# Three kinds of element-wise work moved between GpSimd, ScalarE and VectorE in a fused attention and two-MLP kernel

## The chip, the cores and the metric

The kernel runs on one core of a Trainium2 chip. Measured is the device time of one execution in microseconds (us). The engines: TensorE (PE in the profile, its weight loads PEld), VectorE (DVE), ScalarE (ACT), GpSimd (POOL), and SP, whose queue issues most of the DMAs. Each engine works through its own instructions in the order in which the program gives them, and waits at one until what it needs is there.

## The reference

Three stages, all in fp32: gated linear attention, a mixture of 8 experts with one expert per token, and a dense MLP over all 3072 tokens.

```python
# attention: B=4, H=8, S=768, D=48
f = 1.0 / (1.0 + np.exp(-f_logit))
for t in range(S):
    state = f[:, :, t, :, None] * state + np.einsum('bhd,bhe->bhde', k[:, :, t], v[:, :, t])
    y[:, :, t] = np.einsum('bhd,bhde->bhe', q[:, :, t], state)

# first experts: x (3072, 384), E=8, F=1024; only tokens with x @ w_skip > 0
logits = xc @ w_gate
e_idx = np.argmax(logits, axis=1)
for e in range(E):
    h = np.maximum(xc[mask] @ w1[e], 0.0)
    y[mask] = gate_w[mask, None] * (h @ w2[e])
out[do_compute] = xc + y

# second MLP: F=2048
h = x @ w_in
sp = log1p(exp(h))
g = h * np.tanh(sp)
return g @ w_out
```

## The kernel before, in words

TensorE multiplies in fp32r, a rounded form of fp32. To keep precision every operand is split into a rounded part (hi) and a residual (lo = raw - hi), and each product is three matmuls: hi*hi, hi*lo, lo*hi. So beside TensorE there is much element-wise work: rounding copies and residual subtractions, of the weights (the class `Weights`), of the transposed inputs (`transposed`) and of the hidden values (`split`, `gate`).

*Weights.* They come from HBM by DMA into three stage buffers, a chunk at a time. `Weights.step` handles one piece: for the first experts a chunk has three pieces of 512 columns. ScalarE casts the piece to hi (L123); the residual of the piece before (L108, in `flush`) is issued on the engine that the caller passes in, VectorE if none. With the last piece of a chunk the residual of that piece follows at once, and a new chunk is asked for. The second MLP's weights are wide (64 bit) and need three VectorE instructions more per piece (L129 to L131); their residual is L108 or L135.

*The first experts* (`moe`). Expert 0 is computed in two halves of 128 tokens: `half1` multiplies with the tokens as the stationary operand, `half2` transposes the result back on TensorE and splits it, `layer2` makes the second product. Between them `steps(n)` handles n pieces of weights for later experts. From s = 8 on a loop runs over s = (expert e, slice f of 128 hidden columns): `layer1` for s (L890), `layer2` for s - 3 (L905), at f = 5 and 6 the transposes of the next expert's rows (`make_xT`; one PSUM buffer pt, L849, read by ScalarE in L850 and VectorE in L851), and up to two pieces of weights. `split` (L878 on ScalarE, L879 on VectorE: mhh and mhl) reads each h from PSUM.

*The second MLP* (`moe2`, the second experts). `order` is a list of 96 steps (block b of 512 tokens, slice f of 128 hidden columns); the first 32 steps are blocks 0 and 1. In step s the code issues `layer1` for s (9 matmuls of 512 columns, L1056; three PSUM buffers h), `gate` for s - 5, `read_h` for s, and `layer2` for s - 7 (12 matmuls of 384 columns, L1105). `read_h` copies h out of PSUM to hs (L1068) and starts the activation with a sigmoid on ScalarE; `tanh_sp` does the logarithm and tanh for two or four steps in one go, with a table load before each kind. `gate` makes hs * sp (L1086), its rounded part gh (L1087) and its residual gl (L1088). In steps 3 to 6 the four pieces of block 1's input are transposed, each through pt (L849), with cast and residual on VectorE (L850, L851). Only GpSimd issues the indirect scatters (L224): rows of the first experts, and the four output pieces at the end of a block.

*Which engine.* In `moe`, pieces alternated between VectorE and GpSimd for the residual. In `moe2`, `busy(b, f)` was true for the first 32 steps: there ScalarE copied h and VectorE made gl; later VectorE copied h and GpSimd made gl.

Of the kernel before, what the change touches and what calls it, by code (L numbers as in the profile page):

```python
# [8 lines left out]
F32 = mybir.dt.float32  # L9
# [5 lines left out]
ALU = mybir.AluOpType  # L15
# [842 lines left out]
def moe(tc, A, st, weights, expert_w, pools, work, ps, ys2, rows0, xT0, x0, attn, more, first):  # L858
    nc = tc.nc
# [5 lines left out]
    def load_x(e):  # L865
        xin[e] = load_rows(tc, A, pools, NTOK + e * CAP)
# [29 lines left out]
    def layer2(e, f, halves):  # L896
        _, (w2h, w2l) = expert_w[e]
        weights.need(2 * e + 1, (f + 1) * DM)
        for a in halves:
            if f == 0:  # L900
                ys[e, a] = ys2[e % 2]().tile([128, DM], F32, name="y", tag=f"y{e % 2}", bufs=2)
            hh, hl = hts.pop((e, f, a))
            ws = slice(f * DM, (f + 1) * DM)
            for i, (h, w) in enumerate(((hh, w2h), (hh, w2l), (hl, w2h))):
                nc.tensor.matmul(  # L905
                    ys[e, a], lhsT=h, rhs=w[:, ws],
                    start=(f == 0 and i == 0), stop=(f == NE - 1 and i == 2),
                )
# [3 lines left out]
    def half1(a, g, k, hi, lo, spare):  # L912
        (w1h, w1l), _ = expert_w[0]
        weights.need(0, 4 * (g + 1) * KD * 128)
        if k == 0:
            rows_of[a, g] = ps.tile([128, 512], F32, name="h", tag="h", bufs=3)
        h = rows_of[a, g]
        for i, (w, x) in enumerate(((w1h, hi), (w1h, lo), (w1l, hi))):
            nc.tensor.matmul(  # L919
                h, lhsT=x[:, k, :], rhs=w.rearrange("p (f k t) -> p k f t", k=KD, t=128)[:, k, 4 * g:4 * g + 4, :],  # L920
                start=(k == 0 and i == 0), stop=(k == KD - 1 and i == 2),
            )
        if k == KD - 1:
            r = rows_of[a, g] = spare()
            nc.scalar.copy(r, h)

    def half2(a, g):
        h = ps.tile([128, 512], F32, name="h", tag="h", bufs=3)
        r = rows_of.pop((a, g))
        for i in range(4):  # L930
            nc.tensor.transpose(h[:, i * 128:(i + 1) * 128], r[:, i * 128:(i + 1) * 128], ident)
        for i in range(2):
            hts[0, 4 * g + 2 * i, a], hts[0, 4 * g + 2 * i + 1, a] = split(h[:, i * CAP:(i + 1) * CAP])

    def finish(e, halves):
        for a in halves:
            x = xin[e][:, a, :]
            nc.vector.scalar_tensor_tensor(x[:, 0:DM], ys[e, a], x[:, GATE:GATE + 1], x[:, 0:DM], ALU.mult, ALU.add)
            scatter_rows(tc, "experts", st, U[0:NTOK, :], x[:, POS:POS + 1].bitcast(U32), x)
# [7 lines left out]
    NF = FF // 128  # L947
    LAG = 3
    both = (0, 1)

    def steps(n):
        for i in range(n):
            weights.step(nc.gpsimd if i % 2 else None)

    x0 = (*st["x0T"], st["spare"])
    half1(0, 0, 0, *x0)
# [18 lines left out]
    for f in range(NF):  # L975
        if f == 3:
            half2(0, 1)
            steps(4)
        layer2(0, f, (0,))
    finish(0, (0,))  # L980
    make_xT(0, 1)
    make_xT(1, 0, "h", 3)
    make_xT(1, 1, "h", 3)
    steps(4)
    x1 = [t[:, :, 128:256] for t in xT[0]]
    for g, k in ((0, 0), (0, 1), (0, 2), (1, 0), (1, 1), (1, 2)):
        half1(1, g, k, *x1, spare)
        if (g, k) == (1, 1):
            half2(1, 0)
    for f in range(NF):  # L990
# [7 lines left out]
    for s in range(NF, total + 1):  # L998
        e, f = divmod(s, NF)
        if s < total:  # L1000
            layer1(e, f)
        if s >= NF + LAG:
            e2, f2 = divmod(s - LAG, NF)
            if s < total:
                layer2(e2, f2, both)
                if f2 == NF - 1:
                    finish(e2, both)
                    if e2 + 3 < NE:
                        load_x(e2 + 3)
            else:  # L1010
                for a in both:
                    for f2 in range(NF - LAG, NF):
                        layer2(e2, f2, (a,))
                    if a == 0:
                        first_rows(1)
                    finish(e2, (a,))
                weights.step(nc.gpsimd)
                first()
            if (e, f) == (NE - 1, LAG):
                for j in range(3):  # L1020
                    rows0[j] = load_rows(tc, A, pools, 256 * j)
        if e + 1 < NE and f in (5, 6):
            make_xT(e + 1, f - 5)
        if (e, f) == (NE - 1, NF - 1):
            first_rows(0)
        for i in range(1 if e == 1 and f in (3, 4, 5, 6) else 2):
            if weights.unit() < 2 * min(e + 3, NE):
                weights.step(nc.gpsimd if s % 2 else None)
            elif i == 0 and (NE - 2) * NF <= s < total - 1 and s % 4 < 3:
                weights.step()  # L1030


def moe2(tc, A, st, weights, w2, pools, work, ps, ys2, xTs, rows0):
    nc = tc.nc
# [3 lines left out]
    NF = FF2 // 128  # L1038
    BATCH = 4
    GLAG = 5  # L1040
    LAG = 7
    HF = NF // 2
    order = [(b, f) for h in range(2) for b in range(2) for f in range(h * HF, (h + 1) * HF)]
# [14 lines left out]
                    start=(k == 0 and i == 0), stop=(k == KD - 1 and i == 2),  # L1058
                )

    def busy(b, f):
        return b < 2

    def read_h(b, f):
        h = hp.pop((b, f))
        hs = work.tile([128, TB], F32, name="hs", tag="hs", bufs=7)
        sp = work.tile([128, TB], F32, name="sp", tag="sp", bufs=7)
        (nc.scalar.copy if busy(b, f) else nc.vector.tensor_copy)(hs, h)  # L1068
        nc.scalar.activation(out=sp, in_=hs, func=AF.Sigmoid, scale=-1.0)  # L1069
        hts[b, f] = (hs, sp)  # L1070

# [10 lines left out]
    def gate(b, f):  # L1082
        hs, sp = hts.pop((b, f))
        gh = work.tile([128, TB], F32R, name="gh", tag="gh", bufs=4)
        gl = work.tile([128, TB], F32R, name="gl", tag="gl", bufs=3)
        nc.vector.tensor_tensor(hs, hs, sp, ALU.mult)  # L1086
        nc.vector.tensor_copy(gh, hs)  # L1087
        (nc.vector if busy(b, f) else nc.gpsimd).tensor_tensor(gl, hs, gh.bitcast(F32), ALU.subtract)  # L1088
        gs[b, f] = (gh, gl)

    def layer2(b, fs):
# [44 lines left out]
    steps = NBK * NF  # L1136
    n_test = len(weights.wide_chunks())
    for s in range(-1, steps + LAG):
        if s < 0:
            layer1(0, 0)  # L1140
            work = yield
            rows[0] = rows0[0:2]
            load_block(0)
            load_block(1)
            continue
        b, f = order[s] if s < steps else (NBK, 0)
        if 0 < s < steps:
            layer1(b, f)
        if 0 <= s - GLAG < steps:
            gate(*order[s - GLAG])  # L1150
        if s < steps:
            read_h(b, f)
            if s in (1, 3, steps - 3, steps - 1):
                tanh_sp(s - 1, 2)
            elif s % BATCH == BATCH - 1:
                tanh_sp(s - BATCH + 1, BATCH)
        if LAG <= s < steps + LAG - 2:
            layer2(order[s - LAG][0], [order[s - LAG][1]])
        if s == steps + LAG - 1:
            layer2(NBK - 1, [NF - 2, NF - 1])  # L1160
        if s == 0:
            weights.flush(nc.gpsimd)
        if s == HF - 1 or s >= HF and s % HF != HF - 1:
            weights.step(nc.gpsimd, now=True)
        if s >= 2 * NF and s < steps:
            i, at = divmod(s - 2 * NF, 3)
            if i < n_test and at == 0:
                assert not weights.left() and weights.pend is None
                weights.reload(i)
            elif i < n_test and at == 2:  # L1170
                weights.test(i)
        if s == 2 * NF + 3 * n_test + 1:
            bad = check_values(tc, st, work, weights.stage[2])
        elif s == 2 * NF + 3 * n_test + 3:
            finish_flag(tc, st, ps, work, bad)
        if s < steps:
            nb = 1 if s < HF else b + 1 if s >= 3 * HF else NBK
            at = XT_AT[0] if s < 2 * NF else XT_AT[1]
            if s == NF + 2:
                load_block(2)  # L1180
            if nb < NBK:
                if nb > 2 and f == 5:
                    load_block(nb)
                elif s % HF in at[0:4] and s < HF or nb > 1 and f in (at[4:8] if b == 1 else at):
                    i = at[0:4].index(s) if nb == 1 else at[4:8].index(f) if b == 1 else at.index(f)
                    transposed(
                        tc, st, ps, rows[nb][i // 2][:, i % 2, :], *xTs[nb % 2], slice(i * 128, (i + 1) * 128),
                        copy=nc.vector.tensor_copy,
                    )
# [383 lines left out]
```

## Time and profile before

| what | value |
|---|---|
| three runs | 746.18, 746.66, 751.29 us; median 746.66 |
| profiled execution | 747.82 us; span 746.1 us; mean granted TensorE clock 0.977 |
| TensorE (PE) busy | 715.2 us (96%) |
| VectorE (DVE) busy | 502.8 us (67%) |
| ScalarE (ACT) busy | 508.9 us (68%) |
| GpSimd (POOL) busy | 317.1 us (43%) |

The attention part ends near 178 us, the first experts near 322 us, the second MLP's last matmul near 737 us. The busy table averages over these parts. A line of a timeline gives the start in us, the time taken, the engine, the line and the operation, how many instructions are merged, and in brackets how long the engine had been idle before and what ended that. A wait is put down to the semaphore that came last.

### The profile page before, as it was taken

Reading aid. Unit: us, or ns where it says so; the run is one execution under the profiler, and the core shown is the slowest. Engines: PE = TensorE matmul, PEld = TensorE weight load, DVE = VectorE, ACT = ScalarE, POOL = GpSimd, SP = SyncE. Lnnn points to the kernel's source line nnn. Section 1 sums busy time; section 2 is a strip of 40 time slices with the busy share of each in tenths; the row PEclk is TensorE's granted clock in tenths of the full one; section 3 lists DMA queues with packets and bytes.
Section 4 is the critical chain, followed back from the end, with each engine's and each line's share of the span. In section 5 each row is a group of like instructions: output and inputs, shape, how many; then the busy total and the mean of one; then the engine's idle time right before and its main releaser. Section 6 shows DMA issues by size and latency. Waiting matters only on the chain.

```text
span 746.1 us, 12713 instructions
## 1 busy us (share of the span) xinstructions
PE 715.2 (96%) x4749; PEld 630.0 (84%) x4749; DVE 502.8 (67%) x963; ACT 508.9 (68%) x898; POOL 317.1 (43%) x333
## 2 busy tenths in 40 slices
PE   7999999989999999998999999999999999999995
PEld 3677777667999899987989899899989998898995
DVE  6687967975666767956889886565467544666461
ACT  5788686733666664379788767767787677667681
POOL 4655675663677663120323121432253325224434
PEclk8899999987999999999999999999999999999998
DMA  9999995243788785441223011312132124100001
GB/s 185 213 207 277 234 292 145 87 156 133 218 257 276 248 257 203 145 171 43 85 86 127 1 54 62 140 43 86 43 127 85 50 90 151 50 1 33 11 1 46
DMA packets 39285, 95.50 MB, mean 128 GB/s; under 512 B 3540, under 2 KB 28160, under 8 KB 39216
## 3 DMA queue, kind: packets, MB, share of 16 engines
q1 hardware_dynamic: 35120, 82.71, 39.6%
q0 software_dynamic: 4096, 11.90, 4.3%
q8 instruction: 39, 0.64, 0.4%
q14 instruction: 30, 0.25, 0.1%
HBM read 79.53 MB, written 15.84 MB: 128 GB/s over the span
## 4 chain that ended last, share of the span: by engine, by line
PE 73%; DVE 10%; ACT 7%; DMA 4%; issue 3%; POOL 2%; SPq 0%; POOLq 0%; DVEq 0%; ACTq 0%
PE y L1105 25%; PE h L1056 24%; PE y L905 6%; PE h L890 6%; DVE fb L292 2%; PE ou L431 2%; PE fin L475 2%; PE ou L424 2%; PE pt L849 2%; PE at L373 1%; PE h L919 1%; POOL out L224 1%; DVE g L346 1%; DVE kg L345 1%; DMA kq<-in_kqT 1%
## 5 line engine op out<-in xcount | busy, mean ns | idle before, releaser
L1088 POOL TENSOR_TENSOR gl<-hs,gh 128x512 fp32r<-128x512 f32 x64 | 83.5, 1309 | 157.6 <-DVE gh L1087 131.0
L1086 DVE TENSOR_TENSOR hs<-hs,sp 128x512 f32<-128x512 f32 x96 | 90.9, 947 | 32.7 <-ACT sp L1080 32.7
L1069 ACT ACTIVATE sp<-hs 128x512 f32<-128x512 f32 x96 | 59.6, 628 | 77.3 <-DVE hs L1068 76.1
L1056 PE MATMUL h<-wB,wA 128*128 128x512 f32 x432 | 108.0, 396 | 3.2 <-ACT hs L1068 3.2
L1056 PE MATMUL h<-wB,wB 128*128 128x512 f32 x432 | 109.1, 397 | 0.0
L1105 PE MATMUL y<-wA,gh 128*128 128x384 f32 x384 | 98.4, 337 | 0.0
L1105 PE MATMUL y<-wD,gh 128*128 128x384 f32 x384 | 98.0, 336 | 0.0
L1056 PEld LDWEIGHTS h<-wB,wA 128*128 128x128 f32 x432 | 80.5, 188 | 18.2 <-ACT hs L1068 3.7
L1056 PEld LDWEIGHTS h<-wB,wB 128*128 128x128 f32 x432 | 79.5, 188 | 14.6
L1068 DVE COPY hs<-h 128x512 f32<-128x512 f32 x64 | 44.2, 691 | 67.9 <-PE h L1056 64.5
L1105 PEld LDWEIGHTS y<-wA,gh 128*128 128x128 f32 x384 | 70.8, 190 | 4.4
L1105 PEld LDWEIGHTS y<-wD,gh 128*128 128x128 f32 x384 | 70.0, 188 | 3.7
L1105 PE MATMUL y<-wA,gl 128*128 128x384 f32 x192 | 65.1, 339 | 1.6 <-POOL gl L1088 1.6
L1105 PE MATMUL y<-wD,gl 128*128 128x384 f32 x192 | 64.6, 336 | 0.0
L1076 ACT ACTIVATE sp<-sp,tiny 128x512 f32<-128x512 f32 x96 | 61.8, 713 | 0.3
L1087 DVE CAST gh<-hs 128x512 fp32r<-128x512 f32 x96 | 52.7, 549 | 3.7
L1080 ACT ACTIVATE sp<-sp 128x512 f32<-128x512 f32 x96 | 52.9, 621 | 0.3
L879 DVE SCALAR_TENSOR_TENSOR mhl<-h,mhh 128x256 fp32r<-128x256 f32 x64 | 26.7, 420 | 32.3 <-ACT mhh L878 32.0
L878 ACT ACTIVATE mhh<-h 128x256 fp32r<-128x256 f32 x64 | 24.6, 384 | 34.7 <-PE h L890 25.3
L373 PE MATMUL at<-qh,kh 48*128 48x128 f32 x384 | 35.4, 303 | 4.9 <-POOL qh L359 1.6
L387 POOL TENSOR_SCALAR_AFFINE_SELECT am<-am 128x512 f32<-128x512 f32 x41 | 29.1, 711 | 21.7 <-ACT am L385 21.0
L1105 PEld LDWEIGHTS y<-wA,gl 128*128 128x128 f32 x192 | 36.3, 189 | 2.2 <-POOL gl L1088 2.2
(238 smaller groups left out, 1544.4 us busy)
## 6 DMA issues: line engine op xcount, KB each, us to landing
stage<-in_w SPq DMA_DIRECT2D x64, 768.0 KB
kq<-in_kqT SPq DMA_DIRECT2D x6, 1344.0 KB
rows<-tokens SPq DMA_DIRECT2D x18, 388.0 KB
fb<-in_fT SPq DMA_DIRECT2D x7, 672.0 KB
vb<-in_v SPq DMA_DIRECT2D x7, 576.0 KB
tokens<-zeros SPq DMA_DIRECT2D x4, 776.0 KB
kq<-in_kqT SPq DMA_DIRECT2D x4, 448.0 KB
kq<-in_kqT SPq DMA_DIRECT2D x1, 896.0 KB
```

Source lines behind the costliest of these rows:

```text
L373: nc.tensor.matmul(at[:, j, a * CH:(a + 1) * CH], lhsT=k[r, p, :], rhs=q[r, p, :], start=True, stop=True)
L890: nc.tensor.matmul(h, lhsT=w[:, o:o + 128], rhs=x[:, k, :], start=(k == 0 and i == 0), stop=(k == KD - 1 and i == 2),)
L905: nc.tensor.matmul(ys[e, a], lhsT=h, rhs=w[:, ws], start=(f == 0 and i == 0), stop=(f == NE - 1 and i == 2),)
L1056: nc.tensor.matmul(h, lhsT=w[:, o:o + 128], rhs=x[:, k, :], start=(k == 0 and i == 0), stop=(k == KD - 1 and i == 2),)
L1068: (nc.scalar.copy if busy(b, f) else nc.vector.tensor_copy)(hs, h)
L1069: nc.scalar.activation(out=sp, in_=hs, func=AF.Sigmoid, scale=-1.0)
L1076: nc.scalar.activation(out=sp, in_=sp, func=AF.Ln, bias=st["tiny"])
L1080: nc.scalar.activation(out=sp, in_=sp, func=AF.Tanh, scale=-1.0)
L1086: nc.vector.tensor_tensor(hs, hs, sp, ALU.mult)
L1087: nc.vector.tensor_copy(gh, hs)
L1088: (nc.vector if busy(b, f) else nc.gpsimd).tensor_tensor(gl, hs, gh.bitcast(F32), ALU.subtract)
L1105: nc.tensor.matmul(ys[b][a], lhsT=g[:, a * 128:(a + 1) * 128], rhs=w, start=(first and i == 0), stop=(fs[-1] + 1 in ends and i == len(ins) ...
```

## The change

In `moe`, no caller passes GpSimd any more, so all weight residuals of the loop and of `steps` go to VectorE. Two of the four pieces handled in expert 0's first half are handled later, in the second half. In `moe2`, `gl` is always VectorE's, and `busy` depends on the step: true from step 7 to step 31, so the copies of h in steps 0 to 6 go from ScalarE to VectorE.

```diff
@@ moe
     def steps(n):
         for i in range(n):
-            weights.step(nc.gpsimd if i % 2 else None)
+            weights.step()
...
         if f == 3:
             half2(0, 1)
-            steps(4)
+            steps(2)
         layer2(0, f, (0,))
...
         half1(1, g, k, *x1, spare)
+        if (g, k) == (1, 0):
+            steps(2)
         if (g, k) == (1, 1):
             half2(1, 0)
...
             if weights.unit() < 2 * min(e + 3, NE):
-                weights.step(nc.gpsimd if s % 2 else None)
+                weights.step()
@@ moe2
-    def busy(b, f):
-        return b < 2
-
-    def read_h(b, f):
+    def busy(s):
+        return LAG <= s < 2 * NF
+
+    def read_h(s):
+        b, f = order[s]
         h = hp.pop((b, f))
...
-        (nc.scalar.copy if busy(b, f) else nc.vector.tensor_copy)(hs, h)
+        (nc.scalar.copy if busy(s) else nc.vector.tensor_copy)(hs, h)
...
-        (nc.vector if busy(b, f) else nc.gpsimd).tensor_tensor(gl, hs, gh.bitcast(F32), ALU.subtract)
+        nc.vector.tensor_tensor(gl, hs, gh.bitcast(F32), ALU.subtract)
...
-            read_h(b, f)
+            read_h(s)
```

What this does to an engine's order stands best in three places. (Lines behind the change are numbered 3 higher.)

VectorE at the start of the second MLP (wt is a wide piece of weights; pt is the transposed input, wB its place). Before:

```order
L131 SCALAR_TENSOR_TENSOR wt<-stage_81,wt 128x384
L850 CAST wB_1577<-pt 128x3x128
L851 TENSOR_TENSOR wB_1577<-pt,wB_1577 128x3x128
L850 CAST wB_1577<-pt 128x3x128
L851 TENSOR_TENSOR wB_1577<-pt,wB_1577 128x3x128
L1086 TENSOR_TENSOR hs<-hs,sp 128x512
L1087 CAST gh<-hs 128x512
L1088 TENSOR_TENSOR gl<-hs,gh 128x512
L850 CAST wB_1577<-pt 128x3x128
L851 TENSOR_TENSOR wB_1577<-pt,wB_1577 128x3x128
```

And now:

```order
L131 SCALAR_TENSOR_TENSOR wt<-stage_81,wt 128x384
L1071 COPY hs<-h 128x512 x4
L850 CAST wB_1577<-pt 128x3x128
L851 TENSOR_TENSOR wB_1577<-pt,wB_1577 128x3x128
L1071 COPY hs<-h 128x512
L850 CAST wB_1577<-pt 128x3x128
L851 TENSOR_TENSOR wB_1577<-pt,wB_1577 128x3x128
L1089 TENSOR_TENSOR hs<-hs,sp 128x512
L1090 CAST gh<-hs 128x512
L1091 TENSOR_TENSOR gl<-hs,gh 128x512
L1071 COPY hs<-h 128x512
L850 CAST wB_1577<-pt 128x3x128
```

Seven copies of h now stand in VectorE's queue, the last three each in front of a transposed piece's cast and residual; ScalarE's queue has lost them.

GpSimd behind the second block's outputs (out is the scatter of a finished block, idx the row numbers of a later one):

```order
-L1088 TENSOR_TENSOR gl<-hs,gh 128x512 x15
-L1134 COPY idx<-rows 128x2 x2
-L1088 TENSOR_TENSOR gl<-hs,gh 128x512
+L1137 COPY idx<-rows 128x2 x2
 L224 DMA out<-stage_79,idx 3072x384
 L224 DMA out<-stage_80,idx 3072x384
 L224 DMA out<-stage_79,idx 3072x384
 L224 DMA out<-stage_80,idx 3072x384
```

All 64 gl instructions are gone from GpSimd; the scatters and index copies stay.

VectorE in expert 0's two halves (wC and wD are weights of a later expert, x the first half's output, mxT transposed rows):

```order
+L108 TENSOR_TENSOR wC_2385<-stage_80,wC_2384 128x512
+L938 SCALAR_TENSOR_TENSOR x_2120<-y,x_2120 128x384
+L851 TENSOR_TENSOR mxT_2443<-pt,mxT_2442 128x3x128
+L851 TENSOR_TENSOR mxT_2451<-pt,mxT_2450 128x3x128 x2
 L108 TENSOR_TENSOR wC_2385<-stage_80,wC_2384 128x512 x2
-L938 SCALAR_TENSOR_TENSOR x_2120<-y,x_2120 128x384
-L851 TENSOR_TENSOR mxT_2448<-pt,mxT_2447 128x3x128
-L851 TENSOR_TENSOR mxT_2456<-pt,mxT_2455 128x3x128 x2
-L108 TENSOR_TENSOR wC_2385<-stage_81,wC_2384 128x512
+L108 TENSOR_TENSOR wC_2385<-stage_81,wC_2384 128x512 x3
+L108 TENSOR_TENSOR wD_2377<-stage_79,wD_2376 128x512
 L879 SCALAR_TENSOR_TENSOR mhl<-h,mhh 128x256 x4
```

One residual stands in front of x where two stood, and six stand between the transposed rows and the first mhl where one stood.

## Rows read from the trace of the kernel before

**Rows 1.** TensorE's timeline, 238 to 634 us: start, us taken, instructions merged, idle before.

```profile
245.81 0.55 PE L849 MATMUL pt<-ident,rows 128*128 128x128 f32 x3 [1.85 <-DVE mxT L851]
...
322.74 8.41 PE L1056 MATMUL h<-wB,wA 128*128 128x512 f32 x36
...
334.77 2.33 PE L1056 MATMUL h<-wB,wA 128*128 128x512 f32 x9 [0.89 <-ACT hs L1068]
...
342.16 3.06 PE L1056 MATMUL h<-wB,wA 128*128 128x512 f32 x9 [2.34 <-ACT hs L1068]
...
348.01 2.24 PE L1056 MATMUL h<-wB,wA 128*128 128x512 f32 x9
...
352.17 2.23 PE L1056 MATMUL h<-wB,wA 128*128 128x512 f32 x9
...
555.17 2.33 PE L1056 MATMUL h<-wB,wB 128*128 128x512 f32 x9
...
559.76 2.21 PE L1056 MATMUL h<-wB,wB 128*128 128x512 f32 x9
...
623.48 2.33 PE L1056 MATMUL h<-wB,wB 128*128 128x512 f32 x9
...
627.71 0.44 PE L1105 MATMUL y<-wA,gl 128*128 128x384 f32 x1 [1.55 <-POOL gl L1088]
...
629.54 2.25 PE L1056 MATMUL h<-wB,wB 128*128 128x512 f32 x9
```

**Rows 2.** Windows, TensorE: length, busy (count), granted clock, DMA share, GB/s.

```profile
343.00:347.00 4.00, 4.00 (x14) 0.57 0.30 75
```

**Rows 3.** Timelines of VectorE and GpSimd, 238 to 246 us.

```profile
240.00 4.96 DVE L108 TENSOR_TENSOR wA<-stage,wA 128x512 fp32r<-128x512 f32 x1 [0.77 <-ACT wA L123]
...
238.11 3.81 POOL L108 TENSOR_TENSOR wD<-stage,wD 128x512 fp32r<-128x512 f32 x3
241.86 2.54 POOL L108 TENSOR_TENSOR wA<-stage,wA 128x512 fp32r<-128x512 f32 x2
```

**Rows 4.** ScalarE's timeline, 312 to 352 us.

```profile
341.54 0.56 ACT L1068 COPY hs<-h 128x512 f32<-128x512 f32 x1
```

**Rows 5.** VectorE's timeline, 312 to 352 us.

```profile
331.51 0.56 DVE L850 CAST wB<-pt 128x384 fp32r<-128x384 f32 x1 [6.44 <-PE pt L849]
...
334.99 0.68 DVE L1086 TENSOR_TENSOR hs<-hs,sp 128x512 f32<-128x512 f32 x1
```

**Rows 6.** By line: count, ns least/median/most of one, first and last start, forms.

```profile
L108 DVE TENSOR_TENSOR wA<-stage,wA x11: 677/685/4956, 199.5 to 250.9; 128x512 fp32r<-128x512 f32 x11
...
L1088 DVE TENSOR_TENSOR gl<-hs,gh x32: 691/693/1533, 336.2 to 466.2; 128x512 fp32r<-128x512 f32 x32
...
L1068 DVE COPY hs<-h x64: 682/692/693, 451.6 to 720.6; 128x512 f32<-128x512 f32 x64
```

**Rows 7.** Timelines of VectorE and GpSimd, 612 to 634 us.

```profile
618.58 0.43 DVE L1087 CAST gh<-hs 128x512 fp32r<-128x512 f32 x1
...
619.76 1.30 POOL L1088 TENSOR_TENSOR gl<-hs,gh 128x512 fp32r<-128x512 f32 x1
...
626.38 3.76 POOL L1088 TENSOR_TENSOR gl<-hs,gh 128x512 fp32r<-128x512 f32 x3
```

**Rows 8.** The page's slices: busy tenths of VectorE in 40 slices of 18.7 us.

```profile
DVE  6687967975666767956889886565467544666461
```

**Rows 9.** Timelines of VectorE and TensorE in expert 0's second half.

```profile
188.12 0.68 DVE L108 TENSOR_TENSOR wC<-stage,wC 128x512 fp32r<-128x512 f32 x1
191.49 0.42 DVE L879 SCALAR_TENSOR_TENSOR mhl<-h,mhh 128x256 fp32r<-128x256 f32 x1 [2.69 <-ACT mhh L878]
...
191.97 0.44 PE L905 MATMUL y<-wB,mhl 128*128 128x384 f32 x1
```

**Rows 10.** One round: all engines (PE, PEld, DVE, ACT, POOL); then line 108 (DVE, POOL).

```profile
211.18:228.68 17.50, 17.50 (x128) 17.43 (x128) 10.80 (x20) 11.99 (x27) 13.73 (x12) 1.00 0.73 255
...
211.18:228.68 17.50, 5.76 (x7) 11.74 (x10) 1.00 0.73 255
```

## The prediction, made before the result was known

> **What bounds the kernel now.** I read the busy table first, then TensorE's own timeline for every gap behind the attention part, then the timelines of the engine that each gap names. From 200 us to the tail TensorE is the bound: it runs back to back, and only what makes it wait, or slows its clock, counts. The reader is to see in [rows 1] where its queue breaks. A normal step of the second experts (first layer, then second layer of an older step) takes 352.17 - 348.01 = 4.16 us, so 2.08 a layer. Four places are longer. Before 245.81 it waits for a residual of VectorE's (1.85). Before 334.77 and 342.16 it waits for ScalarE's copy of h (0.89, 2.34). From 555.17 to 559.76 a step takes 4.59, and from 623.48 to 629.54 another takes 6.06, the latter with 1.55 named as a wait for GpSimd's gl. The idle figures are counted from a matmul's modelled end, about 0.2 later than the queue could have gone on, so I price by starts where I can. [rows 2] is the price of the second gap besides the waiting: the mean granted clock of 343 to 347 us is 0.57, so TensorE sat at the lower level (1.2 GHz), after the idle of 0.89 and 2.34, for a loss of 4 x 0.43 = 1.7 us.
>
> **The change part by part.**
>
> *Residuals of the first experts, all on VectorE.* [rows 3]: one residual that takes 0.68 alone took 4.96 from 240.00 to 244.96, while GpSimd ran three residuals and then two, to 244.40. VectorE did not start work until GpSimd let go; the residual of the transposed rows behind it came late, and the one pt buffer held up the next transposes. With GpSimd's residuals gone that blocking has no cause. Gain: the 1.85 and the 0.2 hidden in its count, 2.0 us. Elsewhere in this part TensorE has no gap, so nothing more is to be gained there.
>
> *h copied by VectorE in the first seven steps.* I walk from 322.74, where the second experts' first layers begin, to 348.01, where step 8's begins (25.27 us) [rows 1]. Before, ScalarE had the copies between its table loads and functions, and the copy that step 7's matmuls wait for started only at 341.54 [rows 4]. VectorE meanwhile sat idle for 6.44 us up to 331.51 [rows 5]. Now the copies of steps 0 to 3 run in that idle time, at 0.69 each [rows 6], and step 5 no longer waits. Then VectorE is itself the tight one. Step 4's matmuls start at 331.3, as before (322.74, four layers of 2.08 and some 0.25 for a transpose), and end 2.33 later, at 333.6. From there VectorE has in order: copy of h 0.69; cast and residual of a transposed piece, 0.56 each; gate 0.68 + 0.43 + 0.69; copy 0.69; cast and residual [rows 5 to 7]. That is 5.4 with small gaps, or 5.2 as the next instruction starts a little before the end: done at 338.8 to 339.1, and I take 338.9. The tanh that the gate needs costs nothing: the gate of step 0 began at 334.99 before, with ScalarE further behind. TensorE goes 333.6, transpose, 5's layer, transpose, 6's layer, and at 338.1 stands before the fourth transposes, which need the single pt buffer: a new wait of 0.8. Then 0.25 and 2.08 for step 7 and 2.08 for the first second layer: step 8 starts at 343.3 instead of 348.0. Gain 4.7, the clock's 1.7 in it; that a wait of 0.8 does not lower the clock is supported by the clock staying up after the 1.85 of 245.81. Bounds of the new wait: 0 (it hides) to 2.3 (as large as the old one).
>
> *gl of blocks 2 to 5 on VectorE.* In [rows 7] the cast gh is done at 619.01, but GpSimd first had an older gl at 619.76, and then the four scatters that stand behind it in its queue: this gl follows at 626.38, in a row of three. On VectorE it stands right behind its cast, for 0.69 [rows 6]. The two long steps come down to 4.16: 4.59 and 6.06 give 0.4 + 1.9. The 64 instructions cost VectorE 64 x 0.69 = 44 us over the last 15 slices of 18.7 us, 16% more, where it stands at 4 to 6 tenths [rows 8]; a gate then ends sooner than with GpSimd's 1.3, and the copy of h behind it 0.6 later, with three h buffers and two steps of slack. Price of these: nothing; if the cover failed, each step could lose up to 0.6.
>
> *Two pieces moved.* Behind the second half's transposes VectorE now has six residuals in front of the first mhl, where it had one from 188.12 on: 6 x 0.605 (start to start) ends at 191.75, and mhl starts there and not at 191.49. TensorE takes mhl at 191.97, 0.06 after it ends, so this is on its path: loss 0.24 [rows 9]; bounds 0 and the whole of five residuals, 3.0. The reload of their stage is issued later too; what it brings is cast two batches of pieces on, so I price it at nothing (without that cover casts and residuals come late, for which TensorE does not wait in this part). The two scatters of x on GpSimd come earlier, off the path.
>
> *VectorE's load in the first experts' rounds.* [rows 10]: in one round of 17.50 us VectorE is busy 10.80, of which 5.76 are seven residuals; GpSimd has ten. Seventeen at 0.63 (queued back to back) to 0.68 and the other 5.04 make 15.7 to 16.6: 90 to 95%. It holds, with the waits for casts inside it, but with little to spare when a stage comes late. For the transposed pieces I allow 0.4 over all rounds, with bounds 0 and 8 (2.0 in each of four rounds). Against the change speaks the Trainium skill, Perfetto Trace Analysis, section Optimizing Scalar/DVE Operations: where VectorE is saturated, moving work off to ScalarE or even GpSimd may make sense. The trace agrees as far as 90 to 95% is near full. By that rule the gain at 245 would come back as waits, which is the third case below and its 742.5 us; by the rows it does not.
>
> **Sum**: -2.0 - 4.7 - 0.4 - 1.9 + 0.24 + 0.4 = -8.4 us. Against the profiled execution's own 747.82 that is 739.4; against the median of the three runs shown, 746.66 (1.16 lower), 738.3. I forecast between: 738.8. What a measurement of this kernel can tell from no change is about 1%, here 7.5 us, so the sum lies just past it.
>
> **The rivals.**
> 1. *As summed* (0.64): 737.1 (no new wait of 0.8, no allowance, on the median) to 740.5.
> 2. *The wait at the start moves from ScalarE to VectorE* (0.15): the transposes' wait grows from 0.8 to 2.3, the clock falls again. For it: gates, copies and transposed pieces stand in one queue. Against: 5.2 us of work for 4.5 of TensorE's. Gain there 4.7 - 1.5 - 1.7 = 1.5: about 741.5.
> 3. *VectorE full in the rounds* (0.12): the transposed pieces come late in four rounds, by 0.5 to 2.0 each. For: 90 to 95%. Against: six residuals of GpSimd's kind in a row no longer exist. 740 to 746, say 742.5.
> 4. *Slower than before* (0.05): VectorE's residual costs more than 0.73 on average, where it fills the round ((17.50 - 5.04) / 17), in the 72 residuals of the rounds; each 0.1 above costs 7.2 us, so beyond 0.85 all gain is gone. In the round shown the seven took 5.76 / 7 = 0.82, but beside GpSimd; alone the median is 0.685 and the least 0.677 [rows 6]. At GpSimd's own 11.74 / 10 = 1.17 it would be 31 - 8 above: 770.
> 5. *It does not do what it says* (0.04): the gaps reappear behind the next late thing, rows or stages from DMA; 745 to 747.
>
> Past 739.2 (faster by over 1%) lies three quarters of case 1: 0.48. Within 1% lie the rest of it, cases 2, 3 and 5: 0.47. Slower by more: 0.05. Range for 8 in 10: 737.0 to 743.2, from the low end of case 1 through most of cases 2 and 3.
>
> **What would show it.** In the profile after: no residual on VectorE above 0.8 in the first experts, and no gap of TensorE near 245; the copies of h on VectorE inside the former idle time, step 8's first layer 20.6 us behind step 0's, one gap of about 0.8 before the fourth transposes, and the granted clock at its upper level (2.4 GHz) from 320 us to the tail; no step of blocks 2 to 5 above 4.5; VectorE about 90% busy in the rounds; the first mhl of the second half 0.2 later. I am wrong if gaps before transposes or second layers appear in the rounds, or if the clock falls again near 340.

## The result and the profile after

The changed kernel takes 739.8 us (median of 6 runs, 736.18 to 751.62); the kernel before, run beside it, 747.73 (6 runs, 746.18 to 751.92). The medians lie 7.9 us apart, 1.1%. The ratio of the two kernels is 0.9876, 95% interval 0.9834 to 0.9918: faster by 1.2%, or by 6 to 12 us. This ratio and those below are of means over the executions within 1.5% of their kernel's fastest, which leaves out 751.60 and 751.62 of after here and, further down, the longest of both kernels, one of before at 979.14 among them.

One thing is needed to read the profile: in the attention part, ahead of everything that the change touches, TensorE's clock varies from execution to execution, and the profiled one of after (751.62 us, span 749.8) met it low for longer than the one of before, so the first experts start 14 us later in it (184.47 against 170.27). The page's clock rows, 40 slices of the span in tenths, after and then before:

```profile
PEclk8899589975999999999999999999999999999998
```

```profile
PEclk8899999987999999999999999999999999999998
```

The reader is to see the 5, 7 and 5 of the first ten slices, and that the rest agree. So I compare by stretches of TensorE's own timeline, from its first second-layer matmul of the first experts (L905) on, where both run at the upper level (2.4 GHz), but for 3.4 us in before, inside the window of [rows 2]:

| stretch | before | after | difference |
|---|---|---|---|
| expert 0, first L905 to the first L890 (us) | 17.44 | 18.40 | +0.96 |
| the first experts' rounds, first L890 to the second MLP | 126.00 | 123.89 | -2.11 |
| step 0 to step 8 of the second MLP | 25.27 | 20.70 | -4.57 |
| step 8 to the end of the last matmul | 389.13 | 386.91 | -2.22 |
| all four | 557.84 | 549.90 | -7.94 |

Every edit lies behind the first of these points, so what the change does is to be seen here. In the first row, 0.68 of the 0.96 are waits for rows from DMA, which differ from execution to execution (1.78 in all after, 1.10 before); without them the sum is -8.6. That it comes to the 7.9 us of the medians is chance, as the attention part alone differs by more from one execution to the next; it lies inside the interval of the ratio.

**The rounds.** The windows of each engine (PE, PEld, DVE, ACT, POOL: busy and instructions; granted clock, DMA share, GB/s), before, then after, with one round of after in which VectorE has 28 instructions, and that round again for the residuals (line 108) on VectorE and GpSimd alone:

```profile
196.74:322.74 126.00, 123.99 (x890) 122.87 (x890) 92.47 (x170) 71.44 (x158) 65.62 (x52) 1.00 0.72 236
```

```profile
209.24:333.13 123.89, 123.76 (x889) 122.94 (x889) 104.17 (x209) 71.47 (x158) 14.00 (x13) 1.00 0.72 241
...
223.68:241.18 17.50, 17.50 (x128) 17.44 (x127) 14.53 (x28) 11.72 (x27) 1.99 (x2) 1.00 0.80 264
...
223.68:241.18 17.50, 10.14 (x16) 0.00 (x0) 1.00 0.80 264
```

TensorE is now busy for 123.76 of 123.89: no gap is left, where [rows 1] had 1.85 before 245.81. VectorE has 39 more instructions, which at 0.68 would be 26.5 us, and only 11.7 more time: the residuals that it already had became faster (its 133 other instructions in the rounds take 64.7 us before and 64.5 after, added up). In the round of [rows 10] seven residuals took it 5.76, 0.82 each; here sixteen take 10.14, 0.63 each, and the round leaves it 17% idle. GpSimd has none of them left. (One call at the very end of `moe` still passes GpSimd, as before; its residual falls behind the rounds.) Residuals by line after (count, ns least/median/most, first and last start):

```profile
L108 DVE TENSOR_TENSOR wA<-stage,wA x24: 677/681/686, 212.0 to 264.1; 128x512 fp32r<-128x512 f32 x24
...
L108 DVE TENSOR_TENSOR wD<-stage,wD x18: 680/683/692, 203.4 to 291.7; 128x512 fp32r<-128x512 f32 x18
```

Against the 677/685/4956 of [rows 6], none of these is above 0.692; the longest in the rounds is a wB of 0.748.

**The second MLP's start.** VectorE's timeline after, 330 to 352 us (start, taken, instruction, idle before):

```profile
335.40 0.69 DVE L1071 COPY hs<-h 128x512 f32<-128x512 f32 x1
337.46 0.69 DVE L1071 COPY hs<-h 128x512 f32<-128x512 f32 x1 [1.37 <-PE h L1058]
...
345.65 0.68 DVE L1089 TENSOR_TENSOR hs<-hs,sp 128x512 f32<-128x512 f32 x1
346.37 0.43 DVE L1090 CAST gh<-hs 128x512 fp32r<-128x512 f32 x1
346.83 0.69 DVE L1091 TENSOR_TENSOR gl<-hs,gh 128x512 fp32r<-128x512 f32 x1
347.44 0.68 DVE L1071 COPY hs<-h 128x512 f32<-128x512 f32 x1
348.04 0.55 DVE L850 CAST wB<-pt 128x384 fp32r<-128x384 f32 x1
348.62 0.56 DVE L851 TENSOR_TENSOR wB<-pt,wB 128x384 fp32r<-128x384 f32 x1
```

And TensorE's there:

```profile
333.13 8.41 PE L1058 MATMUL h<-wB,wA 128*128 128x512 f32 x36
...
349.32 0.52 PE L849 MATMUL pt<-ident,rows 128*128 128x128 f32 x3 [0.58 <-DVE wB L851]
...
353.83 2.23 PE L1058 MATMUL h<-wB,wA 128*128 128x512 f32 x9
```

Copies follow each layer at once, in what was the idle time of [rows 5]. The two waits of [rows 1] for ScalarE are gone. One wait is new: the fourth transposes, because the gate of step 0 (1.8 us) and a copy stand in VectorE's queue in front of the cast that frees pt. Step 8 starts 353.83 - 333.13 = 20.70 behind step 0. The clock, 0.57 in [rows 2], stays up through that wait and behind it (TensorE alone):

```profile
342.00:348.00 6.00, 6.00 (x31) 1.00 0.00 0
348.00:352.00 4.00, 3.42 (x18) 1.00 0.02 4
352.00:358.00 6.00, 6.00 (x34) 1.00 0.17 35
```

**The steps behind.** gl is always VectorE's (compare [rows 7]). TensorE's step that took 6.06 in [rows 1] runs from 628.87 to 633.12:

```profile
L1091 DVE TENSOR_TENSOR gl<-hs,gh x96: 691/692/1530, 346.8 to 734.5; 128x512 fp32r<-128x512 f32 x96
```

```profile
628.87 2.33 PE L1058 MATMUL h<-wB,wB 128*128 128x512 f32 x9
633.12 2.25 PE L1058 MATMUL h<-wB,wB 128*128 128x512 f32 x9
```

TensorE names no wait behind 349.32 any more, and in blocks 2 to 5 no step from a first layer to the next is above 4.42; the 4.59 and the 6.06 of [rows 1] are both 4.25. VectorE's own product in the gate (hs * sp, 96 of them; busy time, then mean ns) became shorter as well, before and after:

```profile
L1086 DVE TENSOR_TENSOR hs<-hs,sp 128x512 f32<-128x512 f32 x96 | 90.9, 947 | 32.7 <-ACT sp L1080 32.7
```

```profile
L1089 DVE TENSOR_TENSOR hs<-hs,sp 128x512 f32<-128x512 f32 x96 | 69.7, 726 | 32.9 <-ACT sp L1083 32.8
```

With gl alone moved (below) the mean is 0.73 us too, with the copies alone 0.95. So GpSimd's gl had stretched VectorE's work here as well, by 21 us in all. No wait of TensorE is put down to it, and the prediction had not counted it.

### The profile page after: what moved, and what is told of

Same layout as the page of the kernel before. It is cut to its first block, busy times and chain, and to the rows that moved or that the text cites. A ratio compares the mean times of both kernels' runs of the same rounds, so it can differ in the third digit from the quotient of the medians.

```text
span 749.8 us, 12587 instructions
## 1 busy us (share of the span) xinstructions
PE 728.4 (97%) x4749; PEld 640.1 (85%) x4749; DVE 536.4 (72%) x1077; ACT 505.1 (67%) x891; POOL 174.9 (23%) x226
## 4 chain that ended last, share of the span: by engine, by line
PE 84%; DVE 6%; ACT 3%; issue 3%; POOL 1%; DMA 1%; POOLq 0%; SPq 0%; DVEq 0%; ACTq 0%
PE y L1108 27%; PE h L1058 26%; PE y L905 9%; PE h L890 8%; PE ou L431 3%; PE ou L424 2%; PE fin L475 2%; PE at L373 2%; PE pt L849 2%; DVE fb L292 1%; PE ou L415 1%; PE h L919 1%; PE at L378 1%; DVE kg L345 1%; DVE g L346 1%
## 5 line engine op out<-in xcount | busy, mean ns | idle before, releaser
L1089 DVE TENSOR_TENSOR hs<-hs,sp 128x512 f32<-128x512 f32 x96 | 69.7, 726 | 32.9 <-ACT sp L1083 32.8
L1071 DVE COPY hs<-h 128x512 f32<-128x512 f32 x71 | 48.8, 688 | 40.8 <-PE h L1058 40.6
L1091 DVE TENSOR_TENSOR gl<-hs,gh 128x512 fp32r<-128x512 f32 x96 | 67.4, 702 | 12.8 <-PE y L1108 6.2
L1108 PE MATMUL y<-wA,gl 128*128 128x384 f32 x192 | 64.5, 336 | 0.0
L224 POOL DMA_INDIRECT out<-stage,idx x24 | 23.6, 985 | 123.7 <-ACT stage L1127 61.0
L1090 DVE CAST gh<-hs 128x512 fp32r<-128x512 f32 x96 | 48.8, 509 | 3.3
L373 PE MATMUL at<-qh,kh 48*128 48x128 f32 x384 | 39.3, 330 | 2.9 <-ACT xts L465 0.9
L224 POOL DMA_INDIRECT tokens<-rows x14 | 14.7, 1053 | 108.1 <-DVE rows L938 105.9
L465 ACT COPY xts<-ou 112x256 f32<-112x256 f32 x48 | 18.3, 381 | 31.9 <-PE ou L431 23.4
```

What stands on the lines that cost most here:

```text
L373: nc.tensor.matmul(at[:, j, a * CH:(a + 1) * CH], lhsT=k[r, p, :], rhs=q[r, p, :], start=True, stop=True)
L1071: (nc.scalar.copy if busy(s) else nc.vector.tensor_copy)(hs, h)
L1091: nc.vector.tensor_tensor(gl, hs, gh.bitcast(F32), ALU.subtract)
L1108: nc.tensor.matmul(ys[b][a], lhsT=g[:, a * 128:(a + 1) * 128], rhs=w, start=(first and i == 0), stop=(fs[-1] + 1 in ends and i == len(ins) ...
```

## Experiments

My theory is the prediction's: three independent causes, each removed by one part of the change. Its rivals are that the parts need each other, that the copies help only through the clock, and that VectorE is nearly full in the rounds, so that the first part is gained narrowly or by luck.

### Each part alone

First experts alone: the kernel before, with

```diff
-            weights.step(nc.gpsimd if i % 2 else None)
+            weights.step()
...
-            steps(4)
+            steps(2)
...
+        if (g, k) == (1, 0):
+            steps(2)
...
-                weights.step(nc.gpsimd if s % 2 else None)
+                weights.step()
```

> Only the first experts' part of the change: residuals on VectorE, two pieces moved; second MLP as before. Measured from first matmul to first matmul: the rounds (first L890 to the second MLP's first layer) took 126.0 us before and 123.9 with the whole change. Theory (GpSimd's residuals blocked one of VectorE's): rounds 123.9, no gap of TensorE in them, no residual on VectorE above 0.8 in the rounds; the start of the second MLP (step 0 to step 8) stays at 25.3, the rest at 389. Rival (the gap came from something else, and went with the other parts): rounds 126, with the gap of 1.9.

The copies alone:

```diff
-    def busy(b, f):
-        return b < 2
+    def busy(s):
+        return LAG <= s < 2 * NF
...
-        (nc.scalar.copy if busy(b, f) else nc.vector.tensor_copy)(hs, h)
+        (nc.scalar.copy if busy(s) else nc.vector.tensor_copy)(hs, h)
...
-        (nc.vector if busy(b, f) else nc.gpsimd).tensor_tensor(gl, hs, gh.bitcast(F32), ALU.subtract)
+        (nc.vector if b < 2 else nc.gpsimd).tensor_tensor(gl, hs, gh.bitcast(F32), ALU.subtract)
```

> Only the copies of h of steps 0 to 6 moved to VectorE; residuals and gl as before. Theory: step 0 to step 8 takes 20.7 instead of 25.3 us, granted clock at its upper level throughout, one gap of 0.6 before the fourth transposes; rounds stay at 126.0 and the rest at 389.1. Rival (the lower clock is not a consequence of the waits on ScalarE): only the waits go, and step 0 to 8 takes 22.4 to 22.9.

gl alone:

```diff
-        (nc.vector if busy(b, f) else nc.gpsimd).tensor_tensor(gl, hs, gh.bitcast(F32), ALU.subtract)
+        nc.vector.tensor_tensor(gl, hs, gh.bitcast(F32), ALU.subtract)
```

> Only gl of blocks 2 to 5 moved to VectorE. Theory: step 8 to the last matmul takes 386.9 instead of 389.1 us, no step above 4.5; rounds 126.0, start 25.3 as before. Rival (VectorE waits for tanh, and the copies of h behind gl come late): the two long steps go but others appear, 388 to 391.

Measured, one profiled execution each (762.2, 744.65 and 746.66 us; before beside them 745.54; the totals carry the attention part's clock, so the stretches are read; the row of before is the execution of [rows 1]):

| | rounds | step 0 to 8 | step 8 to end |
|---|---|---|---|
| before | 126.00 | 25.27 | 389.13 |
| first experts alone | **123.72** | 25.20 | 388.42 |
| copies alone | 127.52 | **20.71** | 389.01 |
| gl alone | 126.56 | 25.26 | **387.11** |
| all, after | 123.89 | 20.70 | 386.91 |

Each part moves its own stretch, and where no edit stands the others stay within 0.7 of before, but for the 127.52 (below). The sum of the bold gains is 2.28 + 4.56 + 2.02 = 8.86, less the moved pieces' 0.25 (below) 8.61, against 7.94 + 0.68 of DMA waits = 8.62 for all; with those 0.7 in the stretches it could not be expected to come out so closely. The parts don't need each other. The waits stay where their part is missing. TensorE's, first experts alone:

```profile
350.22 2.36 PE L1058 MATMUL h<-wB,wA 128*128 128x512 f32 x9 [0.84 <-ACT hs L1070]
...
357.61 3.90 PE L1058 MATMUL h<-wB,wA 128*128 128x512 f32 x9 [2.32 <-ACT hs L1070]
...
642.42 0.44 PE L1107 MATMUL y<-wA,gl 128*128 128x384 f32 x1 [0.97 <-POOL gl L1090]
```

Copies alone:

```profile
246.08 0.55 PE L849 MATMUL pt<-ident,rows 128*128 128x128 f32 x3 [1.85 <-DVE mxT L851]
...
340.77 0.52 PE L849 MATMUL pt<-ident,rows 128*128 128x128 f32 x3 [0.58 <-DVE wB L851]
...
624.87 0.44 PE L1106 MATMUL y<-wA,gl 128*128 128x384 f32 x1 [1.56 <-POOL gl L1089]
```

The first has no gap in the rounds and the two old ones at the start; the second has the gap at 246 and the new 0.58 that belongs to the copies. One reading I had not expected is the 127.52: the same gap of 1.85 cost 1.5 more than in before. TensorE's windows behind it, copies alone:

```profile
246.00:250.00 4.00, 3.92 (x20) 0.65 0.61 198
250.00:254.00 4.00, 4.00 (x29) 0.92 0.63 197
```

Here the clock fell to its lower level (1.2 GHz) for 3.4 us, which costs half of that, 1.7; in before and in gl alone it stayed at 1.00 behind the same gap. So against the 123.89 of after the blocking of [rows 3] costs 2.1 in the profiled execution of before and 3.6 in this one; in gl alone (126.56) 0.48 is a wait for DMA.

### Is it the wait or the clock? Three copies

Only steps 0 to 2 copied by VectorE in the kernel before, so that the first of the two old waits goes and the second stays:

```diff
-        (nc.scalar.copy if busy(b, f) else nc.vector.tensor_copy)(hs, h)
+        (nc.scalar.copy if busy(b, f) and not on_vector else nc.vector.tensor_copy)(hs, h)
...
-            read_h(b, f)
+            read_h(b, f, s < 3)
```

> The kernel before with only the first three copies of h on VectorE. ScalarE then still has the copies of steps 3 to 6, two tanh batches in front of step 4's. Theory: the wait before step 5's layer goes (0.9 to 0), the one before step 7's stays or grows (2.3 to 2.7), alone. If one wait of that length keeps the clock up, step 0 to 8 takes 22.6 us; if it lowers it, 24.3. Rival (VectorE not ScalarE decides): 25.3 unchanged.

Measured: 748.81 us; step 0 to step 8 takes 22.65, and TensorE has one wait and no lower clock behind it:

```profile
344.95 2.35 PE L1056 MATMUL h<-wB,wA 128*128 128x512 f32 x9 [2.41 <-ACT hs L1068]
```

```profile
342.00:348.00 6.00, 3.59 (x18) 1.00 0.01 3
348.00:352.00 4.00, 4.00 (x21) 1.00 0.60 197
```

This splits the 4.57: 2.62 for the first of the two waits and the clock, and 1.95 for what the wait that is left costs above the new one of after. Waits of 0.89 and 2.34 lowered the clock in all three executions that had them (before, first experts alone, gl alone); one wait of 2.41 did not in this one. With one execution this is an observation, not a rule: in the same execution the gap of 1.82 in the rounds did lower it, and with a second gap of 0.82 the rounds, whose code is that of before, took 128.32, 4.4 above after.

### What GpSimd's residuals did to VectorE

After, with GpSimd given useless subtractions beside every second residual, which nobody waits for:

```diff
-    def step(self, eng=None, load=True, now=False):
+    def step(self, eng=None, load=True, now=False, beside=None):
...
+            if beside is not None:
+                nc.gpsimd.tensor_tensor(beside, hi.bitcast(F32), hi.bitcast(F32), ALU.subtract)
...
-                weights.step()
+                weights.step(beside=scrap if s % 2 else None)
```

> The changed kernel, and beside it GpSimd does in each odd step, per piece, one subtraction of the same shape (128x512, two operands in SBUF) whose result nobody uses: GpSimd as busy as before, but no work of the kernel on it. Theory (running GpSimd subtractions block VectorE's): residuals on VectorE of 1.2 us and more again, their mean 0.8 to 0.95, VectorE near full in a round, gaps of TensorE of 1 to 5 us in sum, rounds 125 to 129 us. Rival (it was the order or the queue, not the blocking): residuals 0.68, rounds 123.9.

Measured: 752.4 us; rounds 135.10 (after 123.89, before 126.00), beyond what I expected:

```profile
198.77:333.87 135.10, 127.05 (x890) 124.33 (x889) 129.26 (x209) 71.57 (x158) 61.02 (x49) 0.99 0.68 221
```

VectorE does the same 209 instructions in 129.26 and not 104.17, 96% of the stretch. By line (count, busy, mean ns, idle before), here:

```profile
L108 DVE TENSOR_TENSOR wA<-stage,wA 128x512 fp32r<-128x512 f32 x24 | 24.8, 1072 | 0.0
...
L881 DVE SCALAR_TENSOR_TENSOR mhl<-h,mhh 128x256 fp32r<-128x256 f32 x56 | 23.1, 414 | 2.1 <-ACT mhh L880 1.8
```

and in after:

```profile
L108 DVE TENSOR_TENSOR wA<-stage,wA 128x512 fp32r<-128x512 f32 x24 | 15.4, 681 | 0.0
```

Over all 76 residuals VectorE is busy 0.996 us for each, against 0.642 in after (75.7 and 48.8 us in all); the mean length of one is 1.037 against 0.683. mhl, which reads h from PSUM (the memory that TensorE writes its results to), keeps its 0.41. The blocking of [rows 3] is back, three residuals taking 4.27 with GpSimd's two subtractions beside them and, further on, 5.11 with four. So are TensorE's gaps for VectorE's work, six of them, 7.7 in sum and up to 3.83, and behind that one the clock fell once (0.99 in the window):

```profile
243.26 4.27 DVE L108 TENSOR_TENSOR wD<-stage,wD 128x512 fp32r<-128x512 f32 x3
...
265.86 5.11 DVE L108 TENSOR_TENSOR wB<-stage,wB 128x512 fp32r<-128x512 f32 x3
```

```profile
243.87 2.51 POOL L125 TENSOR_TENSOR scrap<-wD 128x512 f32<-128x512 f32 x2
...
266.46 5.41 POOL L125 TENSOR_TENSOR scrap<-wB 128x512 f32<-128x512 f32 x4
```

```profile
271.82 0.55 PE L851 MATMUL pt<-ident,rows 128*128 128x128 f32 x3 [3.83 <-DVE mxT L853]
```

Nobody waits for what GpSimd wrote, so it is its working beside VectorE that costs the time, not the order of the results. The same section of the Trainium skill that spoke against the change (Perfetto Trace Analysis, Optimizing Scalar/DVE Operations) adds that GpSimd and VectorE share a read port of SBUF (the on-chip memory of the operands), which a VectorE operation that uses two ports holds as an exclusive lock, so that moving work between these two might not help. The trace agrees with that conclusion: +25.1 us of VectorE time for the same instructions. Which engine held a port it does not show.

### How full is VectorE? Residuals twice

After, each residual of every second step's weights issued twice, and then (with `weights.twice = True`) each one in the rounds:

```diff
...
-            eng.tensor_tensor(lo, raw, hi.bitcast(F32), ALU.subtract)
+            for _ in range(2 if self.twice and not self.late else 1):
+                eng.tensor_tensor(lo, raw, hi.bitcast(F32), ALU.subtract)
...
+            weights.twice = s % 2 == 0
```

> The changed kernel with the residuals of even steps of the rounds computed twice on VectorE (the second writes the same values): 36 more of 0.63 us. In the changed kernel VectorE is busy 14.5 of a round's 17.5 us, 3.0 free in each of some 4.5 rounds, 13 in all. Theory (what counts is whether VectorE's queue fills the round): 22.7 - 13 = 9 us more, rounds 130 to 134. Rival (waits for ScalarE's casts already fill VectorE's free time): all 22.7 show, rounds 146. Rival (three buffers of h and three steps of slack hide it): 124.

> As the run with half of them, but all 72 residuals of the rounds twice: 45 us more, of which 13 find free time. Theory: rounds 124 + 32 = 153 to 158 us, TensorE waiting before transposes and second layers, VectorE at 95% or more. Rival: 168 (nothing hidden).

Measured: rounds 134.83 with half (753.2 us) and 159.41 with all (771.03 us). Windows of all engines inside the rounds, half, then all:

```profile
220.00:310.00 90.00, 82.76 (x575) 80.61 (x574) 84.41 (x159) 47.98 (x106) 10.76 (x10) 0.98 0.70 223
```

```profile
215.00:315.00 100.00, 78.27 (x490) 74.85 (x489) 96.53 (x170) 44.57 (x97) 8.47 (x8) 0.91 0.60 190
```

At 94 and 97% VectorE is the bound, and TensorE waits for transposed rows, up to 3.91 and 4.08, and with all twice for mhl too, up to 2.29; there the clock fell five times as well, 1.7 each. So the rival "VectorE full" is a real mechanism, and 83% is short of it. The two lie 0.8 and 1.4 us above the ranges given for this theory; the lower clock behind the gaps, 1.7 in the one and 8.5 in the other, is more than that.

### The moved pieces, and the new wait

After with the pieces back in the first half:

```diff
-            steps(2)
+            steps(4)
...
-        if (g, k) == (1, 0):
-            steps(2)
```

> The changed kernel with the two pieces back in their old place: then four residuals, not six, stand in front of the second half's first mhl. From the first second-layer matmul of expert 0's first half to the rounds, less TensorE's waits for DMA in that stretch, the kernel before took 16.33 us; six runs of kernels that have the moved pieces took 16.5 to 16.6, where the clock was up. Theory (the moved pieces cost 0.24): 16.3 here, mhl waiting for ScalarE and not for VectorE. Rival (it is VectorE's taking GpSimd's residuals, not the move): 16.55 still.

Measured: 741.4 us; the stretch that the expectation names takes 16.37. From the second half's first matmul to the first L890, where no execution waits for DMA, TensorE takes 9.91 here and 9.86 to 9.91 in all six executions without the move (before 9.89), and 10.10 to 10.14 in the seven with it (after 10.13). So the move costs 0.24 in the mean. VectorE's timelines show why: not moved (this run), mhl waits for ScalarE,

```profile
192.28 0.68 DVE L108 TENSOR_TENSOR wD<-stage,wD 128x512 fp32r<-128x512 f32 x1
193.84 0.42 DVE L879 SCALAR_TENSOR_TENSOR mhl<-h,mhh 128x256 fp32r<-128x256 f32 x1 [0.88 <-ACT mhh L878]
```

moved (after again), it waits for six residuals:

```profile
202.02 3.09 DVE L108 TENSOR_TENSOR wC<-stage,wC 128x512 fp32r<-128x512 f32 x5
205.03 0.68 DVE L108 TENSOR_TENSOR wD<-stage,wD 128x512 fp32r<-128x512 f32 x1
205.63 0.42 DVE L879 SCALAR_TENSOR_TENSOR mhl<-h,mhh 128x256 fp32r<-128x256 f32 x1
```

After with the transposed piece in front of the gate in the steps before the first second layer:

```diff
-        if 0 <= s - GLAG < steps:
+        if 0 <= s - GLAG < steps and s >= LAG:
             gate(*order[s - GLAG])
...
+        if 0 <= s - GLAG and s < LAG:
+            gate(*order[s - GLAG])
```

> The changed kernel with, in steps 5 and 6, the copy of h and the transposed piece's cast and residual in front of the gate on VectorE instead of behind it. Theory: the gap of 0.6 before the fourth transposes goes and no other comes (gl of step 0 is ready 0.7 before its matmuls): step 0 to 8 takes 20.1 instead of 20.7 us. Rival: the wait goes on to the first second layer, 20.7.

Measured: 734.82 us; step 0 to step 8 takes 19.95 (after 20.70), and the gap is gone: 336.91 - 316.96 by TensorE's starts. The wait was 0.58 in the row and 0.75 in the time.

Both repairs together, timed beside after and before, 12, 13 and 23 runs:

> The changed kernel with both repairs: transposed pieces in front of the gate in steps 5 and 6, and the two pieces back in their old place. Theory: 0.7 + 0.2 = 0.9 us less than the changed kernel from the first half to the last matmul, 549.9 less what the clock does in the first half: 548.3; against the kernel before 8.8 us or 1.2% faster, not to be told from the changed kernel by its time.

> The changed kernel unchanged, timed beside the version with both repairs. Theory: ratio to the kernel before 0.985 to 0.992; rounds 123.7 to 123.9, start 20.7, rest 386.9.

Measured: with both repairs median 741.9 us, ratio to before 0.9889 (0.9851 to 0.9926); after again 741.69, ratio 0.9895 (0.9857 to 0.9933). The four stretches sum to 549.18 with 2.15 of waits for rows (0.36, 1.79), against 549.66 for after with 1.55 (0.56, 0.98): without these waits 547.03 and 548.11, 1.1 apart where 0.9 was expected. Both repairs show in their stretch (19.95, and 9.90 for the pieces), but one microsecond is not to be seen in runs that spread by 26. After again repeats its other stretches: rounds 123.89, start 20.71, rest 386.95. Nothing measured here beats the changed kernel by more than the measurement tells.

## Why the prediction was right

The forecast was 738.8 us with 737.0 to 743.2, faster by over 1% held at 0.48; measured 739.8, faster by 1.2% (0.8 to 1.7). That the total came within 1 us has luck in it: of after's six executions two lie above the range (751.60 and 751.62, at a mean granted clock of 0.957) and one below (736.18, at 0.986), and the forecast has no term for that. The stretches are the better witness: the sum was -8.4, and they give -8.6 without the waits for DMA. By its steps:

- **Residuals, -2.0.** Right: -2.11 in the rounds, no residual above 0.748 in them, no gap at 245. Its cause, the blocking by GpSimd, is shown by the useless subtractions, which bring it back. What the step left out is the clock: behind the same gap it falls in some executions, and then the part is worth 3.6 and more. That -2.0 fits is therefore partly luck, as the execution of before that was read is one in which the clock stayed up.
- **Copies, -4.7.** Right: -4.57. The walk gave a new wait of 0.8 before the fourth transposes and step 8 at 20.6; it was 0.58 and 20.70. That the clock would stay up through it held, behind 0.58 in all seven executions that have this wait; the ground given for it, the clock staying up after the 1.85, did not, since behind that gap it fell in two executions of four.
- **gl, -2.3.** Right: -2.22 with the change, -2.02 for this edit alone. That the four scatters in GpSimd's queue held gl up, and not its own 1.3 us, is read from [rows 7]; no run moved the scatters alone.
- **Moved pieces, +0.24.** Right: 0.24, at the place and for the reason given.
- **VectorE's load, +0.4 allowed.** The mis-sized term. I put 90 to 95% on VectorE in a round; it is 83%, and there was no gap to allow for. I priced 17 residuals at 0.63 to 0.68 each and added 5.04 for the rest; there were 16, at 0.63, and the rest added 4.39 (14.53 - 10.14). The rest did not become faster: the round of after holds 12 such instructions and not 13, and in a fuller queue more of each runs while its neighbour ends. With 0 for this term the sum would have been -8.8.
- **Rivals.** The wait at the start did not grow to 2.3. VectorE was not full; the doubled residuals show that it would have been at some 95%. The slower case needed residuals of over 0.85: with GpSimd busy beside them VectorE is busy 0.996 for each, and the rounds are then 9.1 slower than before. The mechanism was sound and its condition absent, because the edit that loads VectorE is the one that takes GpSimd away.

## What to carry to other kernels

When an engine's instruction takes a multiple of its usual time in the trace, look at what ran beside it before judging how full the engine is: moving a neighbour's work onto it can cost far less than that work's own length (here 26.5 us of instructions for 11.7 us of time). And where one queue feeds TensorE, price an edit by walking that queue in order, since the next wait, its place and its size come out of the walk to 0.2 us. A gap's price has a part that comes and goes, the clock behind it; read more than one execution before a step is priced by it.

## What was not expected of the hardware

- GpSimd's useless subtractions of 128x512 (1.04 to 1.54 us each, mean 1.28) cost VectorE 25.1 us over 36 of them, 0.70 each, more than a residual's own 0.68; VectorE's operation with an operand in PSUM (mhl, 0.414) was not stretched.
- The granted clock behind a wait in a full stretch: after 1.85 or 1.82 it fell in two of four executions, after 0.89 and 2.34 in three of three, after a single 2.41 not, after 3.83 and 3.91 both times, for 3.4 us each time. After gaps of 2.00 (useless subtractions) and 2.29 (all residuals twice) it stayed up, and in the latter execution it fell at gaps of 1.93 to 4.08, five times. What decides between the two cases of 1.85 stays open; the length of the gap alone does not.
- The attention part's clock differs between executions of the same kernel. Over 13 runs of after the total moves by 26 us (735.19 at a mean granted clock of 0.987 to 761.27 at 0.945), about three times what the change is worth. Of both profiled executions of after (751.62, 753.35) the four stretches take 549.90 and 549.66, so what those two lose lies ahead of them.
